# Low parts of the inner S sums taken out of the high-and-low split and written later in four pairs of a mixed FFT and gated MLP kernel

## The chip, the core and the metric

The kernel runs on one core of a Trainium2 chip. The metric is the time of one execution on the device in microseconds (us). The kernel before took 1030.15 us, the median of three runs (1030.04 to 1030.8).

## The reference

Two sublayers are computed from the same input `x` of 2048 rows by 640 columns, and mixed by a gate of one number a row. All arrays are float32.

```python
g = sigmoid((x * gate_w).sum(-1, keepdims=True))
a = dft_seq_re @ (x @ dft_hid_re.T) - dft_seq_im @ (x @ dft_hid_im.T)
b = (gelu(x @ w_gate) * (x @ w_up)) @ w_down
return g * a + (1 - g) * b
```

`w_gate` and `w_up` have 640 by 1728 numbers, `w_down` 1728 by 640, the sequence matrices 2048 by 2048.

## The kernel before

**Products in three passes.** The operands of TensorE (PE) have the type `float32r`. Each is kept as a high part, which ScalarE (ACT) makes by a copy to that type (`high`, L75), and a low part, which VectorE (DVE) makes as operand minus high part (`low`, L78). `mm3` (L86 to L88) issues high by high, high by low and low by high into one bank of 128 by 512 sums.

**Fewer products by sums.** Gate and up projections use a Strassen scheme of 2 by 2 blocks, so that seven block products do the work of eight. Its operands are sums of blocks: `S1` to `S4` of the weights, `T1` to `T4` of `x`. In the main part two hidden blocks are taken as one pair, and the same scheme is used once more on the sums of the outer scheme. `whole_pair` (L509) does that for the pairs p = 2, 3, 4 and 5, that is for the hidden blocks f = 5 to 12 (f = 2p + 1 and 2p + 2). Pair 1 and the blocks before it go through other functions, and so does everything behind the pairs: the down projection (`step_k`), the sequence transform and the last transform.

**What one pair does, in its program order.** `whole_pair` is a generator. It writes the products of one pair and yields a step number now and then, and its caller writes other work at these steps. The names that matter here:

- `va`, `xa` are two banks of running sums, `v00`, `v01`, `v10` and `X[..]` are banks that are copied from them by ACT (`seed`, L443), so that the sum can go on in two places. In the profile they read `pva`, `pxa`, `pv` and `px`.
- `s1[..]` (in the profile `s`) are copies of such banks in SBUF; DVE adds `v..` to them (`plus`, L530) and ACT applies the gelu (L533).
- `chain_parts` (L229) writes, at step 3, the sums of the raw weights of one block into `ws{f}r` (DVE, L241 to L245). It returns a function that writes the high part `ws{f}h` (ACT, 128 by 1024), the low part `ws{f}l` (DVE, 128 by 1024) and the same for a small sum `wd`. The caller calls it for the first block of the pair at step 7, and for the second at step 16.
- `fifth_parts` (L284) writes four small sums `fs` of the two blocks' `S1` (L290 to L293) at step 7, and its own returned function splits them into `fh` at step 10. `fh` is first used behind step 23.
- `load_cross(3, i)` (L326) loads 512 KB from memory into `xx`, at the steps 7, 10 and 16. SP issues it.
- At step 19 the caller issues loads for other stages (`extras`: sums of the down weights in `sum_wd`, with tiles `dr`, `da`, sums `d0s` to `d5s` and the store `wsd`; and rows of `x` for the gate, tiles `xz`). Their DVE work is written at the steps 29 and 38. The raw weights of the next pair are loaded at step 23 (`wa`, `wb`).

**Who sets the order.** Inside a pair only PE's order is fixed to that of the program (`in_order(PE)`). On ACT, DVE and SP a scheduler orders the instructions at build time by its own estimate of when each can run. In the trace each engine runs its list just as it stands, so that an instruction that waits holds up all behind it.

**Buffers.** Nearly all large tiles share one pool of 48 buffers of 4 KB a partition (tag `s4`): the sums and their high and low parts, the `xx` loads, the raw weights and the hidden activations `s5{f}`. A tile gets a buffer that the scheduler takes for free at that point of its plan, and its first write waits, by semaphores, until the last use of the buffer's former tile is over. For `s5{f}` the last use is a store to memory: `keep` (L332) has POOL store each finished 128 by 512 tile to `hA` or `hT`, 256 KB each. These stores come in a row at the end of every pair.

Of the kernel before, what the change touches and what calls it, by code (L numbers as in the profile page):

```python
# [30 lines left out]
def kernel(  # L31
# [33 lines left out]
    def slot(dt, shape, name):  # L65
        return pool.tile(shape, dt, tag="s4", name=name, bufs=48)

    def mtile(dt, name):
        return pool.tile([P, T], dt, tag="m", name=name, bufs=12)
# [4 lines left out]
    def high(hi, raw):  # L74
        nc.scalar.activation(hi, raw, AF.Copy)  # L75

    def low(hi, lo, raw):
        nc.vector.tensor_tensor(lo, raw, hi.bitcast(F32), op=ALU.subtract)  # L78

    def split(hi, lo, raw):  # L80
        high(hi, raw)
        low(hi, lo, raw)

    def mm3(ps, lhs, rhs, first, last):
        (lh, ll), (rh, rl) = lhs, rhs
        nc.tensor.matmul(ps, lh, rh, start=first, stop=False, skip_group_check=True)  # L86
        nc.tensor.matmul(ps, lh, rl, start=False, stop=False, skip_group_check=True)  # L87
        nc.tensor.matmul(ps, ll, rh, start=False, stop=last, skip_group_check=True)  # L88
# [39 lines left out]
    def at(hilo, i):  # L128
        h, l = hilo
        return h[:, i], l[:, i]  # L130

    def copy(src, name):
        m = mtile(F32, name)
        nc.scalar.activation(m, src, AF.Copy)
        return m
# [49 lines left out]
    def wchunk(name):  # L185
        return slot(F32, [P, 8, P], f"{name}r"), slot(F32R, [P, 8, P], f"{name}h"), slot(F32R, [P, 8, P], f"{name}l")

    def wsmall(dt, name):
        return pool.tile([P, 2, P], dt, tag="w", name=name, bufs=6)
# [40 lines left out]
    def load_raw(f):  # L230
        ra, rb = slot(F32, [P, 8, P], f"wa{f}"), wsmall(F32, f"wb{f}")
        nc.sync.dma_start(ra, wf[f - 1, :, :8])
        nc.sync.dma_start(rb, wf[f - 1, :, 8:])
        return ra, rb

    def chain_parts(f, raw, W):

        ra, rb = raw
        sm, *c = wchunk(f"ws{f}")
        g01, g23, u23 = ra[:, 0:2], ra[:, 2:4], ra[:, 5:7]  # L240
        tt(sm[:, 0:2], rb, u23, op=ALU.add)  # L241
        tt(sm[:, 4:6], g01, rb, op=ALU.subtract)
        tt(sm[:, 2:4], sm[:, 0:2], g01, op=ALU.subtract)
        tt(sm[:, 6:8], g23, sm[:, 2:4], op=ALU.subtract)
        tt(rb[:, 1], ra[:, 4], ra[:, 7], op=ALU.subtract)  # L245
        d = wsmall(F32R, f"wd{f}")
        W["raw"] = sm[:, 0:2]

        def parts():
            split(*c, sm)  # L250
            split(d[:, 0], d[:, 1], rb[:, 1])
            W["D"] = d[:, 0], d[:, 1]
            for i in range(2):
                for k in range(4):
                    W[f"S{k + 1}", i] = at(c, 2 * k + i)

        return parts

    def plain_parts(f, ra):
        a = slot(F32R, [P, 2, 4, P], f"wp{f}")  # L260
        split(a[:, 0], a[:, 1], ra[:, 4:8])
        W = {"g5": (a[:, 0, 0], a[:, 1, 0]), "u5": (a[:, 0, 3], a[:, 1, 3])}
        for i in range(2):
            W["A22", i] = a[:, 0, 1 + i], a[:, 1, 1 + i]
        return W
# [61 lines left out]
    def load_cross(J, i):  # L327
        tcross[J, i] = slot(F32R, [P, 2, T], f"xx{J}{i}")
        nc.sync.dma_start(tcross[J, i].bitcast(F32), xtd[J][:, {1: 0, 4: 1, 2: 2}[i]])
# [178 lines left out]
    def whole_pair(p, WP, Ws, raws):  # L508


        f = 2 * p + 1
        b = {J: {"b11": at(Bs[0][J, 1], 0), "b21": at(Bs[0][J, 1], 1), "b22": at(Bs[1][J, 1], 1), "t3": at(Bs[1][J, 1], 0)} for J in (1, 2)}
        b[3] = {"b11": at(Bs[0]["T1"], 0), "b21": at(Bs[0]["T1"], 1), "b22": at(Bs[1]["T1"], 1), "t3": at(Bs[1]["T1"], 0)}
        for J in (1, 2):
            for i in (1, 2, 4):
                c = tcross.pop((J, i))
# [5 lines left out]
        def prod(ps, i, a, b, tp):  # L522
            for d in range(2):
                mm3(ps, Ws[i][a, d], at(Bs[tp][b], d), False, True)

        def fifth(ps, i, w, t, tp):
            mm3(ps, Ws[i][w], at(Bs[tp][5], t), False, True)

        def plus(a, c):
            tt(a, a, c, op=ALU.add)  # L530
# [4 lines left out]
        def state(i, tp):  # L535
            s2[i, tp] = copy(X[i, tp], f"s2{f + i}_{tp}")
# [32 lines left out]
        plus(xa_, sx)  # L569
        X[1, 1] = xa_  # L570
        s1[1, 1] = copy(xa_, f"s111{p}")
        fifth(v01, 0, "g5", 0, 1)
        plus(s1[0, 1], v01)
        yield 13
# [7 lines left out]
        yield 16  # L582
        fifth(va, 1, "g5", 0, 1)
        plus(s1[1, 1], va)
        prod(X[0, 0], 0, "S2", "T2", 0)
        state(0, 0)
        plus(s1[1, 1], sv)
# [7 lines left out]
        for i in (1, 2, 4):  # L595
            c = tcross.pop((3, i))
# [399 lines left out]
    B, tiles, load, piece, tsum, his, lows = load_x(0)  # L996
# [27 lines left out]
    with in_order(ACT, DVE, PE, mybir.EngineType.SP):  # L1024
# [14 lines left out]
        B, tiles, load, piece, tsum, his, lows = load_x(1)  # L1039
# [50 lines left out]
    for f in (1, 2):  # L1090
        s5 = pair(F32, f"s5{f}")
        work = [gate_up(f, W, Bs[tp], tp, s5[:, tp]) for tp in range(2)]
        for step in range(7):
# [5 lines left out]
            if (f, step) == (2, 0):  # L1099
                raws = load_raw(3), load_raw(4)  # L1100
# [10 lines left out]
    Ws = [plain_parts(3 + i, raws[i][0]) for i in range(2)]  # L1111
    for i in (1, 2):
        for J in (2, 1):
            load_cross(J, i)
    chain_parts(3, raws[0], Ws[0])()
    p, f = 1, 3
    for J in (2, 1):
        load_cross(J, 4)
# [2 lines left out]
    for i in range(2):  # L1121
        s5 = pair(F32, f"s5{f + i}")
        work = [chain(f + i, Ws[i], Bs[tp], tp, s5[:, tp], X[i, tp], s1[i, tp]) for tp in range(2)]
        for step in range(4):
            for w in work:
                next(w)
            if (i, step) == (0, 0):
                chain_parts(f + 1, raws[1], Ws[1])()
            if (i, step) == (0, 1):
                xc[3] = cross_loads(3)  # L1130
            if (i, step) == (0, 3):
                t3[3] = cross_sums(3, xc[3])
            if (i, step) == (1, 1):
                split(Bs[1]["T1"][0][:, 0], Bs[1]["T1"][1][:, 0], t3[3])
            if (i, step) == (0, 1):
                for do in extras(1, 2):
                    do()
            if (i, step) == (0, 2):
                nraws = load_raw(f + 2), load_raw(f + 3)
            if (i, step) == (1, 0):  # L1140
                raws = nraws
                WP = pair_parts(2, raws[0][0], raws[1][0])
            if (i, step) == (1, 1):
                Ws = [plain_parts(f + 2 + i, raws[i][0]) for i in range(2)]
                for J in (2, 1):
                    load_cross(J, 1)
            if (i, step) == (1, 2):
                load_cross(2, 2)
            if (i, step) == (1, 3):
                load_cross(1, 2)  # L1150
    for p in range(2, NK):
        f = 2 * p + 1
        more = p < NK - 1
        for J in (2, 1):
            load_cross(J, 4)
        with in_order(PE):
            for u in whole_pair(p, WP, Ws, raws):
                if u == 3:
                    parts = [chain_parts(f + i, raws[i], Ws[i]) for i in range(2)]
                if u == 7:  # L1160
                    parts[0]()
                    parts.append(fifth_parts(p, *Ws))
                    load_cross(3, 1)
                if u == 10:
                    WP[3] = parts[2]()
                    load_cross(3, 2)
                if u == 16:
                    parts[1]()
                    load_cross(3, 4)
                if u == 19:  # L1170
                    todo = extras(1, 2)
                if u == 23 and more:
                    nraws = load_raw(f + 2), load_raw(f + 3)
                if u == 29:
                    for do in todo[:1]:
                        do()
                    todo = todo[1:] + extras(p > 2, 2)
                if u == 38:
                    for do in todo:
                        do()  # L1180
                if more:
                    if u == 47:
                        nWP = pair_parts(p + 1, nraws[0][0], nraws[1][0])
                    if u == 56:
                        nWs = [plain_parts(f + 2, nraws[0][0])]
                        for J in (2, 1):
                            load_cross(J, 1)
                    if u == 62:
# [88 lines left out]
    for i, (j, ri, b, sp) in enumerate(cseq):  # L1277
# [20 lines left out]
        if not b:  # L1298
# [17 lines left out]
            if lst:  # L1316
# [4 lines left out]
                for d in range(2):  # L1321
                    c = sv["c11", d]
# [76 lines left out]
    for i, (tp, b, p) in enumerate(useq[: 3 * ND]):  # L1399
# [95 lines left out]
    for t in range(2):  # L1495
        parts = 2 if t else 1
# [74 lines left out]
```

## Time and profile before

| | us |
|---|---|
| median of three runs | 1030.15 |
| the profiled execution, whole | 1027.66 |
| its span, first to last instruction | 1025.8 |
| PE busy | 1016.0 |
| DVE busy | 807.0 |
| ACT busy | 489.3 |
| POOL busy | 140.7 |

Times in views of the trace count from the start of the span. Pair 2 runs at about 145 to 190 us, pair 3 from 190 to 241, pair 4 from 241 to 291, pair 5 from there on. A row of a timeline is: start, duration, engine, line, operation, out<-in, shapes, and in brackets the idle time of the engine just before it and what ended it. Matmuls follow each other every 0.227 us at full clock and each is drawn 0.39 us long, so an unbroken row of them overlaps; PE busy time close to the span means that there are few gaps. Line numbers are those of the kernel before; in the changed kernel they are 4 to 12 higher.

### The profile page before, as it was taken

How to read it: one execution, taken by the hardware profiler on the slowest of the kernel's cores; microseconds unless marked ns; L12 is line 12 of the kernel's file. 1: busy time of each engine (PE TensorE's matmuls, PEld its weight loads, DVE VectorE, ACT ScalarE, POOL GpSimd, SP SyncE). 2: the span in 40 equal slices, each digit the busy share in tenths (PEclk: the TensorE clock that was granted, in tenths of full speed). 3: DMA queues.
4: the chain of work that ended last, by engine and by line, in shares of the span. 5: the costliest groups of instructions: out<-in, count | busy, mean ns of one | idle time of the engine just before them, and what ended most of it. 6: DMA issues, size and time to landing. Idle time of an engine off the chain costs nothing.

```text
span 1025.8 us, 13092 instructions
## 1 busy us (share of the span) xinstructions
PE 1016.0 (99%) x4488; PEld 838.5 (82%) x4488; DVE 807.0 (79%) x1134; ACT 489.3 (48%) x654; POOL 140.7 (14%) x251
## 2 busy tenths in 40 slices
PE   9999999999999999999999999999999999999998
PEld 7888888787888888888888888888888888888887
DVE  6998797778785958976898976796598769697784
ACT  5445365454455547566355343443444345365430
POOL 0123131212121200100010011102100200021013
PEclk9999999999999999999999999999999999999999
DMA  8368697878698988867856679667966777897748
GB/s 300 120 211 290 248 326 269 298 258 308 235 336 310 301 285 278 282 257 254 322 190 237 212 244 331 228 216 259 324 231 215 269 270 286 292 323 217 276 92 134
DMA packets 87666, 265.00 MB, mean 258 GB/s; under 512 B 11088, under 2 KB 19312, under 8 KB 87600
## 3 DMA queue, kind: packets, MB, share of 16 engines
q1 hardware_dynamic: 65392, 194.47, 55.6%
q0 software_dynamic: 22064, 69.50, 19.8%
q8 instruction: 35, 0.57, 0.2%
q14 instruction: 31, 0.25, 0.1%
q10 hardware_dynamic: 144, 0.20, 0.1%
HBM read 194.38 MB, written 69.75 MB: 257 GB/s over the span
## 4 chain that ended last, share of the span: by engine, by line
PE 81%; issue 13%; POOL 4%; DMA 1%; DVE 1%; ACT 0%; POOLq 0%; DVEq 0%; ACTq 0%
PE pX L86 3%; PE pX L87 3%; PE pX L88 3%; PE pL L87 3%; PE pL L88 3%; PE pL L86 3%; PE pZ L88 2%; PE pZ L87 2%; PE pZ L86 2%; PE pV L87 2%; PE pV L88 2%; PE pV L86 2%; POOL hA L332 2%; POOL hT L332 1%; PE pR L87 1%
## 5 line engine op out<-in xcount | busy, mean ns | idle before, releaser
L75 ACT ACTIVATE ch<-csa 128x1024 fp32r<-128x1024 f32 x32 | 34.0, 1063 | 85.7 <-DVE csa L815 69.2
L75 ACT ACTIVATE ch<-cra 128x1024 fp32r<-128x1024 f32 x32 | 33.9, 1058 | 47.7 <-DVE cl L78 22.4
L78 DVE TENSOR_TENSOR cl<-crb,ch 128x1024 fp32r<-128x1024 f32 x32 | 39.1, 1221 | 16.3 <-ACT ch L75 14.7
L78 DVE TENSOR_TENSOR cl<-cra,ch 128x1024 fp32r<-128x1024 f32 x32 | 39.1, 1223 | 15.5 <-ACT ch L75 10.2
L88 PE MATMUL pL<-ch,xal 128*128 128x512 f32 x128 | 49.8, 389 | 0.0
L87 PE MATMUL pL<-cl,xah 128*128 128x512 f32 x128 | 49.8, 389 | 0.0
L86 PE MATMUL pL<-ch,xah 128*128 128x512 f32 x128 | 49.3, 389 | 0.0
L75 ACT ACTIVATE ch<-crb 128x1024 fp32r<-128x1024 f32 x32 | 33.8, 1057 | 25.0 <-PE pL L87 8.6
L78 DVE TENSOR_TENSOR cl<-csb,ch 128x1024 fp32r<-128x1024 f32 x32 | 39.2, 1224 | 3.1 <-ACT ch L75 1.2
L332 POOL DMA_DIRECT2D hA<-s x48 | 26.1, 544 | 104.7 <-DVE s L685 71.8
L78 DVE TENSOR_TENSOR cl<-csa,ch 128x1024 fp32r<-128x1024 f32 x32 | 39.0, 1220 | 1.2 <-ACT ch L75 0.8
L75 ACT ACTIVATE ch<-csb 128x1024 fp32r<-128x1024 f32 x32 | 34.0, 1063 | 9.3 <-DVE csb L818 5.8
L78 DVE TENSOR_TENSOR kl<-kw,kh 128x1024 fp32r<-128x1024 f32 (+1 forms) x26 | 31.4, 1209 | 5.8 <-ACT kh L75 5.8
L684 ACT ACTIVATE s<-s 128x512 f32<-128x512 f32 x20 | 12.7, 633 | 48.5 <-DVE s L530 33.0
L75 ACT ACTIVATE kh<-kw 128x1024 fp32r<-128x1024 f32 (+1 forms) x26 | 27.1, 1042 | 11.1 <-DVE kw L873 7.1
L928 POOL DMA_DIRECT2D out<-ks x12 | 6.5, 540 | 166.7 <-DVE ks L927 166.1
L332 POOL DMA_DIRECT2D hT<-s x48 | 26.0, 541 | 20.1 <-DVE s L703 5.5
L814 DVE TENSOR_TENSOR csa<-cra 128x512 f32<-128x512 f32 x32 | 21.9, 685 | 8.2 <-DMA wsu<-u2s 4.7
L86 PEld LDWEIGHTS pL<-ch,xah 128*128 128x128 f32 x128 | 24.0, 188 | 5.0
L87 PEld LDWEIGHTS pL<-cl,xah 128*128 128x128 f32 x128 | 24.0, 188 | 5.0
L88 PEld LDWEIGHTS pL<-ch,xal 128*128 128x128 f32 x128 | 24.0, 188 | 5.0
L1273 POOL DMA_DIRECT2D uA<-c x8 | 4.3, 541 | 170.2 <-DVE c L1360 170.0
(3120 smaller groups left out, 3442.1 us busy)
## 6 DMA issues: line engine op xcount, KB each, us to landing
cra<-in_ct SPq DMA_DIRECT2D x64, 512.0 KB, 4.4
crb<-in_ct SPq DMA_DIRECT2D x64, 512.0 KB, 5.3
xx<-xtd SPq DMA_DIRECT2D x42, 512.0 KB, 5.2
hA<-s POOLq DMA_DIRECT2D x48, 256.0 KB, 4.8
hT<-s POOLq DMA_DIRECT2D x48, 256.0 KB, 5.8
kr<-hA SPq DMA_DIRECT2D x24, 512.0 KB, 7.4
kr<-hT SPq DMA_DIRECT2D x24, 512.0 KB, 6.2
ux<-uA SPq DMA_DIRECT2D x24, 512.0 KB, 5.0
```

What stands on the lines that cost most here:

```text
L75: nc.scalar.activation(hi, raw, AF.Copy)
L78: nc.vector.tensor_tensor(lo, raw, hi.bitcast(F32), op=ALU.subtract)
L86: nc.tensor.matmul(ps, lh, rh, start=first, stop=False, skip_group_check=True)
L87: nc.tensor.matmul(ps, lh, rl, start=False, stop=False, skip_group_check=True)
L88: nc.tensor.matmul(ps, ll, rh, start=False, stop=last, skip_group_check=True)
L332: nc.gpsimd.dma_start(to[:, i], src)
L684: nc.scalar.activation(s2, s2, AF.Gelu_apprx_tanh)
L814: tt(s1[:, 0], r1[:, 1], r1[:, 0], op=ALU.subtract)
L928: nc.gpsimd.dma_start(out[2 * tp + t, e], src)
L1273: nc.gpsimd.dma_start(to[:, i], src)
```

## The change

The function that `chain_parts` returned is cut in two, one for the high parts and one for the low parts. In the four calls of `whole_pair`:

- step 7: high parts of the first block, and `load_cross(3, 1)` as before;
- step 12, which is new and lies just ahead of the matmuls of `fifth(v01, ..)`: low parts of the first block, and `load_cross(3, 2)`, which stood at step 10;
- step 13: the four small sums of `fifth_parts`, which stood at step 7;
- step 16: high and low parts of the second block and `load_cross(3, 4)`, as before;
- step 17, which is new: the split of `fifth_parts`' sums, which stood at step 10.

Pair 1 calls both functions one behind the other, as before. No operation is added or taken away.

```diff
-        def parts():
-            split(*c, sm)
-            split(d[:, 0], d[:, 1], rb[:, 1])
+        def highs():
+            high(c[0], sm)
+            high(d[:, 0], rb[:, 1])
+
+        def lows():
+            low(*c, sm)
+            low(d[:, 0], d[:, 1], rb[:, 1])
             W["D"] = d[:, 0], d[:, 1]
...
-        return parts
+        return highs, lows
...
         s1[1, 1] = copy(xa_, f"s111{p}")
+        yield 12
         fifth(v01, 0, "g5", 0, 1)
         plus(s1[0, 1], v01)
         yield 13
...
         plus(s1[1, 1], va)
+        yield 17
         prod(X[0, 0], 0, "S2", "T2", 0)
...
                 if u == 7:
-                    parts[0]()
+                    parts[0][0]()
+                    load_cross(3, 1)
+                if u == 12:
+                    parts[0][1]()
+                    load_cross(3, 2)
+                if u == 13:
                     parts.append(fifth_parts(p, *Ws))
-                    load_cross(3, 1)
-                if u == 10:
+                if u == 16:
+                    for do in parts[1]:
+                        do()
+                    load_cross(3, 4)
+                if u == 17:
                     WP[3] = parts[2]()
-                    load_cross(3, 2)
-                if u == 16:
-                    parts[1]()
-                    load_cross(3, 4)
```

The order of PE's instructions is the same in both kernels. Those of ACT, DVE and SP move, and buffers are given out in another order. The rows below are the built program's. In brackets stand the semaphores that an instruction waits for: `DMASW` is the landing of a DMA that POOL issued (a store), `DMAHW` the landing of one that SP issued (a load), the others are engines; the number behind a tile's name is its number in the program.

ACT in pair 2, behind the copy `s1002` (that is `s1[0, 0]`), before:

```order
L75 ACTIVATE wd6_1413<-wb6_1155 128x128 [waits DMAHW0_49,DVE_49]
L443 ACTIVATE pv102_1457<-pva2_1376 128x512 [waits PE_49,Activation_49]
L533 ACTIVATE s1002_1434<-s1002_1434 128x512 [waits DVE_49]
L75 ACTIVATE fh2_1459<-fs2_1440 128x512 [waits DMAHW3_49,DVE_49]
L134 ACTIVATE s1012_1469<-px012_1428 128x512 [waits DMASW5_49,DMASW2_49,DVE_49]
L443 ACTIVATE px102_1474<-pxa2_1377 128x512 [waits PE_49,Activation_49]
L75 ACTIVATE ws6h_1406<-ws6r_1405 128x1024
```

The same place now:

```order
L75 ACTIVATE ws6h_1406<-ws6r_1405 128x1024 [waits DMASW5_49,DMASW0_49,DVE_49]
L447 ACTIVATE pv102_1450<-pva2_1376 128x512 [waits PE_49,Activation_49]
L537 ACTIVATE s1002_1434<-s1002_1434 128x512 [waits DVE_49]
L75 ACTIVATE wd6_1413<-wb6_1155 128x128 [waits DMAHW0_49]
L447 ACTIVATE px102_1462<-pxa2_1377 128x512 [waits PE_49,Activation_49]
L134 ACTIVATE s1012_1457<-px012_1428 128x512 [waits DMASW1_49,DVE_49]
```

The high part of the second block, `ws6h`, moved from behind the copies `pv102` and `px102` to ahead of both, and it now waits for stores: its buffer is the one that `s53` had. In the pairs 3, 4 and 5 `ws8h`, `ws10h` and `ws12h` moved to the same place, but wait for no store. `fh` moved behind the copies in all four pairs.

SP in pair 3, from the load behind `xx14` on, before:

```order
L329 DMA xx31_1865<-xtd3_128 128x1024 [waits DMAHW5_49,DMAHW1_49,PE_49]
L721 DMA da2_1937<-in_wd 128x256 [waits DMAHW2_49]
L233 DMA wb9_1960<-in_wf 128x256 [waits DMAHW3_49]
L233 DMA wb10_1964<-in_wf 128x256 [waits DMAHW4_49,DVE_49,Activation_49]
L329 DMA xx32_1882<-xtd3_128 128x1024
L721 DMA da3_2001<-in_wd 128x256 [waits DMAHW6_49,DVE_49]
L329 DMA xx34_1921<-xtd3_128 128x1024 [waits DMAHW7_49]
L720 DMA dr2_1936<-in_wd 128x1024 [waits DMAHW0_49,PE_49]
L765 DMA xz6_1940<-in_xz 128x640 [waits DMAHW1_49,PE_49]
```

The same place now:

```order
L333 DMA xx31_1858<-xtd3_128 128x1024 [waits DMASW4_49,DMAHW1_49,DMASW0_49,DVE_49]
L333 DMA xx32_1889<-xtd3_128 128x1024 [waits DMAHW2_49,PE_49,Activation_49]
L333 DMA xx34_1918<-xtd3_128 128x1024 [waits DMAHW3_49,DMASW7_49,DMASW5_49]
L727 DMA da2_1937<-in_wd 128x256 [waits DMAHW4_49]
L233 DMA wb9_1960<-in_wf 128x256 [waits DMAHW5_49]
L233 DMA wb10_1964<-in_wf 128x256 [waits DMAHW6_49,DVE_49,Activation_49]
L727 DMA da3_2001<-in_wd 128x256 [waits DMAHW7_49,DVE_49]
L726 DMA dr2_1936<-in_wd 128x1024 [waits DMAHW0_49,PE_49]
L771 DMA xz6_1940<-in_xz 128x640 [waits DMAHW1_49,PE_49]
```

`xx31` now has the buffer that `s55` had and `xx34` that of `s56`, so both wait for stores at the head of SP's list, and everything behind them waits with them. Before, `ws7l` (DVE) had the buffer of `s55`; it has another now and waits for no store. `xz6` waits for `DMAHW1`, which in both kernels is the landing of `xx31`. Pair 4 has the same shape with `xx31`, `xx34`, `s57`, `s58` and `xz10`.

DVE in pair 3, where the sums `d2s`, `d3s` of the down weights stand among the adds that PE needs, before and now:

```order
L714 TENSOR_TENSOR d2s_1994<-dr2_1936,d2s_1994 128x256 [waits DVE_49]
L530 TENSOR_TENSOR s57_1794<-s57_1794,px003_1808 128x512 [waits DMAHW5_49,Activation_49]
L711 TENSOR_TENSOR d3s_2049<-da3_2001,dr3_2000 128x256 [waits DMAHW6_49,DMAHW5_49,PE_49]
L712 TENSOR_TENSOR d3s_2049<-dr3_2000,da3_2001 128x256
L530 TENSOR_TENSOR pza3_1967<-pza3_1967,sz3_1977 128x512 [waits Activation_49]
```

```order
L720 TENSOR_TENSOR d2s_1994<-dr2_1936,d2s_1994 128x256 [waits DVE_49]
L534 TENSOR_TENSOR s57_1794<-s57_1794,px003_1808 128x512 [waits Activation_49]
L717 TENSOR_TENSOR d3s_2049<-da3_2001,dr3_2000 128x256 [waits DMAHW5_49,DMAHW7_49,DMASW0_49,DVE_49]
L718 TENSOR_TENSOR d3s_2049<-dr3_2000,da3_2001 128x256
L719 TENSOR_TENSOR d3s_2049<-d3s_2049,dr3_2000 128x256 [waits DVE_49]
L772 ISA xz8_2004,z_68<-xz8_2004,gwb_69 128x640 [waits DMAHW6_49]
```

`d3s` now has the buffer of `d2s`, which has that of `xz6`. So `d2s` cannot start before `xz6` was used, and `d3s` not before `d2s` is stored (`DMASW0`). The adds to `pza` and `pz01`, for which PE waits, stand behind `d3s`. In pair 4 `d5s`, `d4s` and `xz10` stand in the same way.

More of the change, by code (lines that the diff above doesn't have):

```diff
@@ L1114 @@
             load_cross(J, i)
-    chain_parts(3, raws[0], Ws[0])()
+    for do in chain_parts(3, raws[0], Ws[0]):
+        do()
     p, f = 1, 3
@@ L1127 @@
             if (i, step) == (0, 0):
-                chain_parts(f + 1, raws[1], Ws[1])()
+                for do in chain_parts(f + 1, raws[1], Ws[1]):
+                    do()
             if (i, step) == (0, 1):
@@ L1160 @@
                 if u == 7:
-                    parts[0]()
-                    parts.append(fifth_parts(p, *Ws))
-                    load_cross(3, 1)
-                if u == 10:
+                    parts[0][0]()
[4 more added lines that the diff above has]
+                if u == 13:
+                    parts.append(fifth_parts(p, *Ws))
+                if u == 16:
+                    for do in parts[1]:
+                        do()
+                    load_cross(3, 4)
+                if u == 17:
                     WP[3] = parts[2]()
-                    load_cross(3, 2)
-                if u == 16:
-                    parts[1]()
-                    load_cross(3, 4)
                 if u == 19:
```

## The prediction

> **What bounds the kernel now.** First the page's table of engines, then the list of waits for PE.
>
> ```profile
> PE 1016.0 (99%) x4488; PEld 838.5 (82%) x4488; DVE 807.0 (79%) x1134; ACT 489.3 (48%) x654; POOL 140.7 (14%) x251
> PE px L86 <- ACT px L443: 4.6, 2, 2.3
> ```
>
> PE is busy for 1016.0 of 1025.8 us. As the change gives PE the same instructions in the same order, it can move the time only through gaps of PE and through its clock. The list of waits shows one group worth having: PE waited twice for a bank copied by ACT, 4.6 us together. The timelines of PE, DVE and ACT show where.
>
> ```profile
> 203.46 0.50 PE L86 MATMUL px<-xx,vq 128*128 128x512 f32 x1 [2.27 <-ACT px L443]
> 253.24 0.50 PE L86 MATMUL px<-xx,vq 128*128 128x512 f32 x1 [2.29 <-ACT px L443]
> 198.42 1.23 DVE L78 TENSOR_TENSOR ws7l<-ws7r,ws7h 128x1024 fp32r<-128x1024 f32 x1 [2.85 <-DMA hT<-s]
> 201.37 0.69 DVE L530 TENSOR_TENSOR px<-px,sx 128x512 f32<-128x512 f32 x1
> 202.34 0.58 ACT L134 ACTIVATE s<-px 128x512 f32<-128x512 f32 x1
> 202.82 0.59 ACT L443 ACTIVATE px<-pxa 128x512 f32<-128x512 f32 x1
> 248.19 1.23 DVE L78 TENSOR_TENSOR ws9l<-ws9r,ws9h 128x1024 fp32r<-128x1024 f32 x1 [2.81 <-DMA hT<-s]
> ```
>
> One gap lies in pair 3 and one in pair 4, at the same instruction. Read backwards: PE's matmul into `px10` starts when ACT has copied that bank (202.82 + 0.59); the copy stood behind `s<-px`, which needed DVE's add of 201.37; and DVE was late because `ws7l` waited 2.85 us for a store to `hT`, since its buffer had belonged to `s55`. The gap is a wait for a buffer whose old content is still being stored.
>
> The windows show what the second gap cost besides (the last row is the core's span and mean clock):
>
> ```profile
> 254.00:256.00 2.00, 2.00 (x6) 1.51 (x5) 2.00 (x4) 1.66 (x4) 0.00 (x0) 0.54 1.01 375
> 256.00:258.00 2.00, 2.00 (x7) 1.59 (x6) 1.64 (x3) 0.76 (x2) 0.00 (x0) 0.60 1.00 395
> core 0: 1025.8 us, clock 0.998
> ```
>
> The granted clock (third number from the end) fell to 0.54 and 0.60 in two windows of 2 us, that is 0.92 + 0.80 = 1.7 us lost. The first gap, as long, had no such stretch: the mean clock of the span is 0.998, and 1.7 of 1025.8 us is all of that.
>
> **What the change removes.** In the new order `px10` is copied ahead of `s1[0, 1]`, and `ws7l` and `ws9l` have buffers that wait for no store. So both gaps go, and the slow stretch with them: 2.27 + 2.29 + 1.7 = 6.3 us. Were that all, the kernel would be faster. But the stores are as late as before; the tiles that now get their buffers are others, and I follow what these hold up.
>
> **What it adds in pair 2.** Now `ws6h` waits for the last store of `s53`, and it stands on ACT ahead of the copy `pv10`.
>
> ```profile
> 152.44 0.39 PE L86 MATMUL pv<-xx,vq 128*128 128x512 f32 x1
> 148.02 1.04 ACT L75 ACTIVATE ws5h<-ws5r 128x1024 fp32r<-128x1024 f32 x1
> 150.65 0.58 ACT L443 ACTIVATE pv<-pva 128x512 f32<-128x512 f32 x1 [0.39 <-PE pva L88]
> L332 POOL DMA_DIRECT2D hT<-s x1: 540/540/540, 148.0 to 148.0; - x1
> DMA to landing us min/median/max: 7.3/7.3/7.3
> 156.50 1.23 DVE L78 TENSOR_TENSOR ws6l<-ws6r,ws6h 128x1024 fp32r<-128x1024 f32 x1 [1.06 <-ACT s L533]
> ```
>
> That store was issued at 148.03 and landed 7.3 us later, at 155.3. With an allowance of 0.1 for the wake-up ACT begins `ws6h` at 155.4; 1.0 for it (as `ws5h`) and 0.58 for `pv10` give 157.0. PE wanted `pv10` at 152.44 and had it since 151.2. So PE stands still for about **4.6 us**. Queued behind `ws6h` on ACT are also the gelu, `px10` and three copies; on DVE `ws6l` (1.23 us) runs once `ws6h` is there, ahead of the add to `px01`, four small sums and four adds. PE wants bank `px00` again for S3 after 24 matmuls (24 x 0.227 = 5.4 us) from 157.0, at 162.4; the ACT chain of some eleven instructions, with two gelus that need those adds, reaches the copy that frees it at about 163.3. That is **0.8 us** more. Pair 2 costs 5.4 us; bounds are a store that lands 2 us earlier or 1 us later (xx32's 512 KB now move beside it): 3.4 to 6.4.
>
> **What it adds in pair 3.** SP's list begins with `xx31`, which waits for `s55`, and `xx34`, which waits for `s56`. The times below are those of before; pair 2's delay moves all of them alike.
>
> ```profile
> L332 POOL DMA_DIRECT2D hT<-s x1: 540/540/540, 193.6 to 193.6; - x1
> DMA to landing us min/median/max: 8.0/8.0/8.0
> L329 SPq DMA_DIRECT2D xx<-xtd x1: 319/319/319, 194.4 to 194.4; - x1
> DMA to landing us min/median/max: 7.0/7.0/7.0
> 202.86 0.88 SPq L765 DMA_DIRECT2D xz<-in_xz  x2
> 209.36 0.83 DVE L766 CUSTOM_DVE_ANT_0 xz<-xz,gwb 128x640 f32<-128x640 f32 x1 [1.47 <-DMA xz<-in_xz]
> 210.87 0.42 DVE L711 TENSOR_TENSOR d2s<-da,dr 128x256 f32<-128x256 f32 x1 [0.67 <-PE pze L88]
> 213.45 0.55 POOL L715 DMA_DIRECT2D wsd<-d2s  x1 [19.27 <-DVE d2s L714]
> ```
>
> `s55` landed at 198.4 (the row of `ws7l`), so `xx31` is issued there and not at 194.42; `s56` landed at 193.64 + 8.0 = 201.6, and only then come `xx34`, `da2`, `wb9`, `wb10`, `da3`, `dr2`. `xz6` cannot go before `xx31` has landed, 7.0 us behind its issue: 205.4 and not 202.86. With the same flight it lands 2.5 us later, so DVE handles it at 211.8. `d2s` and its store follow as before but without the 0.67 us for PE: 213.45 + 2.5 - 0.7 = 215.2 for the issue. DVE then stops at `d3s` until that store has landed, L us later.
>
> ```profile
> DMA to landing us min/median/max: 2.9/3.6/6.9
> 216.99 0.43 DVE L711 TENSOR_TENSOR d3s<-da,dr 128x256 f32<-128x256 f32 x1 [1.40 <-PE pza L88]
> 219.34 0.70 DVE L530 TENSOR_TENSOR pz<-pz,sz 128x512 f32<-128x512 f32 x1
> 220.07 0.60 ACT L625 ACTIVATE s<-pz 128x512 f32<-128x512 f32 x1 [0.82 <-DVE pz L530]
> 221.55 0.39 PE L86 MATMUL pz<-x122h,ws7h 128*128 128x512 f32 x1
> ```
>
> The first of these rows is for the six `wsd` stores (123 to 272 us). From the start of `d3s` to the end of ACT's copy of `pz01` it took 3.7 us; with one small sum more in between (0.34) and the wake-up, PE can go on 4.1 us behind the landing: 215.2 + L + 4.1. PE arrives there at 221.55 - 2.27 = 219.3, its old gap being gone. The new gap is therefore L itself: 2.9 to 6.9 us. I take the median, **3.6**. Should the queue, which stood still meanwhile, deliver `xz6` with a flight of 3.7 and not 6.5, it would be 0.8; that is the lower end.
>
> **Pair 4** goes the same way, one pair on:
>
> ```profile
> 252.63 0.85 SPq L765 DMA_DIRECT2D xz<-in_xz  x2
> 259.04 0.82 DVE L766 CUSTOM_DVE_ANT_0 xz<-xz,gwb 128x640 f32<-128x640 f32 x1 [1.36 <-DMA xz<-in_xz]
> 272.65 0.39 PE L86 MATMUL pz<-x122h,ws9h 128*128 128x512 f32 x1
> ```
>
> `xx31` goes at 248.1 (the store that `ws9l` waited for), `xz10` 7.0 later at 255.1 and not at 252.63; DVE handles it at 261.5, the store of `d4s` is issued 3.4 later as in pair 3, at 264.9, and PE needs the result at 272.65 - 2.29 - 1.7 = 268.7: 264.9 + L + 4.1 - 268.7 = L + 0.3. With the median this is **3.9 us**, bounds 1.1 to 7.2. In pair 5 `xx32` waits for a store of `s59`, but no down-weight sums stand behind it, and nothing of PE's does: nothing.
>
> **Clock.** Three new gaps of 4.6, 3.6 and 3.9 us stand where two of 2.3 us gave one slow stretch of 1.7. I count two such stretches, 3.4 us; bounds are none and three, 0 to 5.1. [...]
>
> **Sum.** 5.4 + 3.6 + 3.9 + 3.4 - 6.3 = +10.0 us. The profiled execution took 1027.66 us, 1.9 more than its span, and the median of the runs is 2.5 above that; the difference is added to the median: 1030.15 + 10.0 = 1040.1, forecast **1040 us**. Three conditions carry it: the buffers as the built program gives them, stores as slow as in the trace, and L near its median.
>
> **Rivals.**
> - *Only pair 2's wait is left*: SP's loads, held back while the stores land, then fly faster, and the `d3s` and `d5s` waits are over before PE comes. 5.4 + 1.7 - 6.3 = +0.8: 1031, from 1028 to 1033. For it: pair 3's lower end is 0.8. Against it: flights of 6 to 7 us in every such burst of the trace.
> - *The long end*: L is 6.9 us, as it was for the very store of `d2s`. 5.4 + 6.9 + 7.2 + 5.1 - 6.3 = +18.3: 1048.
> - *Faster*: in pair 2 the last store of `s53` lands before PE comes for `pv10`. It would have to land by 150.8, 4.5 us earlier than in the trace, as ACT needs 1.6 us behind it; then the two old gaps are gained and, with pairs 3 and 4 hidden, 1030.15 - 6.3 + 0.8 = 1024.5. Against it: the stores before and behind this one took as long (the median of the six `hT` stores around it is 7.9 us).
>
> ```profile
> hT<-s POOLq DMA_DIRECT2D x6, 256.0 KB, 7.9
> ```
>
> - *The change doesn't reach the old wait*: DVE still holds `ws7l` first in its list and stalls there. Against it: its buffer now comes from `xx22`, which PE had finished. It would give 1030 to 1035.
>
> **How the numbers follow.** Forecast 0.56 (own range 1034 to 1046), only pair 2 0.20, the long end 0.16, faster 0.06, the old wait 0.02. 0.2% is 2.1 us, about what a measurement of this kernel can tell from no change. Faster than 1028.1: the fourth case and a little of the second, 0.08. Between: most of the second and the last, 0.13. Slower: 0.79. The range for 8 times in 10 takes in the forecast, most of the second case and the lower half of the third: 1029.5 to 1047.
>
> **What would show it.** In the changed kernel's list of waits PE should no longer wait for ACT's `px` at `L86` in pairs 3 and 4. It should wait once for `pv` at about 152 us, with ACT's `ws6h` idle before it by a store to `hT`; and twice for ACT's `s` ahead of `pz<-x122h`, with DVE's `d3s` and `d5s` idle by the store `wsd`. The forecast is wrong if `ws6h` starts before 151, if `xz6` lands early enough that `d2s` is stored by the time PE reaches S4, or if stores land 2 us sooner throughout.

## The result, and the profile after

The changed kernel took 1040.53 us, the median of four runs (1036.54 to 1041.49); the kernel before, in the runs beside it, 1030.47 us (1030.04 to 1030.96). The ratio is 1.009, with a 95% interval from 1.0063 to 1.0117. The change made the kernel about 1% slower. The profiled execution of the changed kernel was the shortest of its four, 1036.54 us with a span of 1034.7.

The page's table of engines (busy us, share of the span, instructions):

```profile
PE 1019.0 (98%) x4488; PEld 840.7 (81%) x4488; DVE 807.6 (78%) x1134; ACT 489.1 (47%) x654; POOL 140.7 (14%) x251
```

The list of waits of PE (us in total, times, the longest):

```profile
PE pz L86 <- ACT s L631: 5.7, 2, 3.2
PE pv L86 <- ACT pv L447: 4.6, 1, 4.6
```

The old group, PE waiting for ACT's copy of `px`, is gone. Two new groups stand in its place, with three waits. PE's timeline shows where they lie:

```profile
157.45 0.80 PE L86 MATMUL pv<-xx,vq 128*128 128x512 f32 x1 [4.65 <-ACT pv L447]
228.48 0.50 PE L86 MATMUL pz<-x122h,ws7h 128*128 128x512 f32 x1 [3.18 <-ACT s L631]
279.81 0.50 PE L86 MATMUL pz<-x122h,ws9h 128*128 128x512 f32 x1 [2.48 <-ACT s L631]
```

One gap in each of the pairs 2, 3 and 4, 10.3 us together; pair 5 has none. The first is explained by two rows of ACT:

```profile
155.86 1.06 ACT L75 ACTIVATE ws6h<-ws6r 128x1024 fp32r<-128x1024 f32 x1 [5.58 <-DMA hT<-s]
156.82 0.58 ACT L447 ACTIVATE pv<-pva 128x512 f32<-128x512 f32 x1
```

ACT stood still for 5.58 us ahead of `ws6h`, until a store to `hT` had landed. The copy `pv10` was next in its list, and PE started when that was done. For the second gap the rows of DVE, POOL and ACT belong together (pair 3, in order of time):

```profile
216.08 0.82 DVE L772 CUSTOM_DVE_ANT_0 xz<-xz,gwb 128x640 f32<-128x640 f32 x1 [4.63 <-DMA xz<-in_xz]
219.53 0.55 POOL L721 DMA_DIRECT2D wsd<-d2s  x1 [19.67 <-DVE d2s L720]
224.42 0.42 DVE L717 TENSOR_TENSOR d3s<-da,dr 128x256 f32<-128x256 f32 x1 [4.69 <-DMA wsd<-d2s]
227.83 0.60 ACT L631 ACTIVATE s<-pz 128x512 f32<-128x512 f32 x1 [4.99 <-DVE pz L534]
```

DVE handles `xz6` at 216.08, POOL stores `d2s` at 219.53, and DVE does nothing for 4.69 us until that store has landed and `d3s` may overwrite the buffer. The adds to `pza` and `pz01` are queued behind it, ACT waits for them, and PE for ACT. Pair 4 repeats it with `d4s` and `d5s`:

```profile
267.01 0.82 DVE L772 CUSTOM_DVE_ANT_0 xz<-xz,gwb 128x640 f32<-128x640 f32 x1 [3.52 <-DMA xz<-in_xz]
270.45 0.54 POOL L721 DMA_DIRECT2D wsd<-d4s  x1 [17.55 <-DVE d4s L720]
275.75 0.43 DVE L717 TENSOR_TENSOR d5s<-da,dr 128x256 f32<-128x256 f32 x1 [4.54 <-DMA wsd<-d4s]
```

The windows of the trace, cut where the granted clock changes, show what each gap cost besides (the granted clock is the third number from the end):

```profile
157.44:160.85 3.41, 3.40 (x8) 2.75 (x9) 3.41 (x9) 2.38 (x5) 0.00 (x0) 0.50 0.70 226
229.12:232.53 3.41, 3.41 (x10) 2.64 (x9) 3.21 (x9) 1.70 (x3) 0.10 (x1) 0.50 0.55 160
280.32:283.73 3.41, 3.41 (x9) 2.65 (x9) 3.12 (x9) 1.57 (x2) 0.00 (x0) 0.50 0.53 149
```

Each gap is followed by 3.41 us at half clock, in which PE does the work of 1.7. So the list of waits and the clock nearly make up the difference: 4.65 + 3.18 + 2.48 + 3 x 1.7 = 15.4 us of new loss, less the 6.3 that went, is +9.1, and the spans differ by 1034.7 - 1025.8 = 8.9. (Both sums leave something out; see **What went** below.)

### The profile page after: what moved, and what is told of

It reads as the page before. It is cut to its first block, busy times and chain, and to the rows that moved or that the text cites. A ratio compares the mean times of both kernels' runs of the same rounds, so it can differ in the third digit from the quotient of the medians.

```text
span 1034.7 us, 13095 instructions
## 1 busy us (share of the span) xinstructions
PE 1019.0 (98%) x4488; PEld 840.7 (81%) x4488; DVE 807.6 (78%) x1134; ACT 489.1 (47%) x654; POOL 140.7 (14%) x251
## 4 chain that ended last, share of the span: by engine, by line
PE 79%; issue 15%; POOL 4%; DVE 1%; DMA 1%; ACT 0%; POOLq 0%; DVEq 0%
PE pX L86 3%; PE pX L87 3%; PE pX L88 3%; PE pL L86 3%; PE pL L87 3%; PE pL L88 3%; POOL hT L336 2%; PE pZ L86 2%; PE pZ L87 2%; PE pZ L88 2%; POOL hA L336 2%; PE pV L86 2%; PE pV L87 2%; PE pV L88 2%; PE pY L86 1%
## 5 line engine op out<-in xcount | busy, mean ns | idle before, releaser
L75 ACT ACTIVATE kh<-kw 128x1024 fp32r<-128x1024 f32 (+1 forms) x26 | 27.0, 1040 | 10.6 <-DVE kw L879 6.7
```

## The experiments

The diffs are against the changed kernel. In them, `behind(a, b)` tells the scheduler to keep the instruction `a` behind `b` on their engine; it adds no wait of its own. `last()` is the instruction written last. As the scheduler plans anew, buffers may be given out anew too, so each expectation names those that matter. The ratios are to 13 runs of the kernel before on the same chip for each half of the table; the median of these is 1029.56 us for `a_ws6h`, `d_lows34`, `d_lows_h` and `c_lows_only`, and 1029.47 for the other four.

| run | median us | ratio to before, 95% interval | PE's gaps over 1 us in the pairs 2 to 5 (profiled execution) |
|---|---|---|---|
| a_ws6h | 1036.27 | 1.0062, 1.0045 to 1.0079 | 1.83, 3.39, 4.32 |
| d_lows34 | 1028.72 | 0.9992, 0.9983 to 1.0001 | 4.85 |
| d_lows_h | 1023.86 | 0.9943, 0.9929 to 0.9958 | 1.90 |
| c_lows_only | 1038.60 | 1.0085, 1.0070 to 1.0100 | 1.57, 4.09, 3.44, 1.52 |
| c_fifth_only | 1042.92 | 1.0138, 1.0109 to 1.0166 | 4.91, 1.16, 1.17, 5.36, 1.15, 1.61 |
| after_again | 1040.41 | 1.0111, 1.0080 to 1.0141 | 5.83, 4.27, 2.94 |
| a_h | 1024.32 | 0.9953, 0.9938 to 0.9968 | 1.42 |
| e_late6 | 1020.67 | 0.9921, 0.9897 to 0.9945 | none |

### Pair 2: the wait of ws6h moved behind the copies (a_ws6h)

```diff
         def highs():
             high(c[0], sm)
+            if (f - 1) // 2 in (2,) and f % 2 == 0:
+                behind(last(), marks["px10"])
...
         X[1, 0] = seed(xa_, f"px10{p}")
+        marks["px10"] = last()
```

> The changed kernel, with one instruction moved on ACT in pair 2 alone: ws6h, the high part of the second block, is held behind the copy px10 (and so behind pv10, too). It keeps the buffer of s53; in the pairs 3 and 4 buffers and order stay those of the changed kernel. Theory (three gaps with three causes of their own; in pair 2 it is the copy pv10 queued behind ws6h's wait for the store): the 4.65 us gap at pv<-xx,vq and the 1.7 us lost at half clock behind it go, the gaps at pz<-x122h,ws7h and pz<-x122h,ws9h stay at 2 to 5 us each: 1040.5 - 6.3 = 1034, from 1033 to 1036. Rival (the wait only moves: gelu, px00's copy and the adds behind ws6h are then late in its place): PE waits 4 us or more a little later in pair 2, at S3, and the time stays at 1039 to 1041.

Measured: 1036.27 us, 4.3 less than the changed kernel. ACT's row of `ws6h` in the timeline:

```profile
157.75 1.06 ACT L75 ACTIVATE ws6h<-ws6r 128x1024 fp32r<-128x1024 f32 x1 [3.16 <-DMA hT<-s]
```

PE's list of waits:

```profile
PE pz L86 <- ACT s L643: 7.7, 2, 4.3
PE px L86 <- ACT s L143: 1.8, 1, 1.8
```

`ws6h` still waits for the store, and starts no sooner. But `pv10` now stands ahead of it, and the gap of 4.65 us at `pv<-xx,vq` is gone. What the wait holds up now are the copies of `s`, and PE meets it at S3, for 1.8 us. Both expectations saw a part of it: the theory is right on the gap, the rival on the direction, though not on the size. The time is 0.3 above the theory's range, as it had no term for this.

### Pairs 3 and 4: is it d3s, or SP's held loads? (d_lows34)

```diff
         def lows():
             low(*c, sm)
+            if (f - 1) // 2 in (3, 4):
+                behind(last(), marks["px01"])
...
         plus(X[0, 1], sx)
+        marks["px01"] = last()
```

> The changed kernel, with one instruction moved on DVE in each of the pairs 3 and 4: the low part of the first block's sums (ws7l, ws9l) is held behind the add to px01. The buffers that follow from it: xx31 and xx34 still get those of s55 and s56 (s57 and s58 in pair 4), so that SP's list is held as in the changed kernel; but d2s gets xx31's and d3s fh3's, so that neither waits for xz6 nor for the store wsd (d4s and d5s alike). Pair 2 stays as it is. Theory (the gaps of the pairs 3 and 4 are d3s and d5s waiting for their neighbours' stores; SP's hold alone costs nothing): both gaps and the half clock behind them go, 3.2 + 2.5 + 2 x 1.7 = 9.1: 1040.5 - 9.1 = 1031.4, from 1030 to 1034, with the 4.65 us gap of pair 2 left. Rival (it is SP's held loads, with xz6 and the down weights landing late): the gaps at pz<-x122h stay at 2 us or more in both pairs, and the time at 1037 to 1041.

Measured: 1028.72 us, 11.8 less than the changed kernel and below the theory's range. The 9.1 us came from the shortest execution; the second profile of the changed kernel (below) has 4.27 + 2.94 us of gaps in these pairs and 1.5 + 3.1 us lost to half clock behind them, 11.8. The whole list of PE's waits in the pairs is now one line:

```profile
PE pv L86 <- ACT pv L458: 4.8, 1, 4.8
```

The timelines of pair 3 have SP's `xx31`, DVE's `xz6`, POOL's store of `d2s`, and DVE's `d3s`:

```profile
205.56 0.32 SPq L344 DMA_DIRECT2D xx<-xtd  x1
217.68 0.83 DVE L784 CUSTOM_DVE_ANT_0 xz<-xz,gwb 128x640 f32<-128x640 f32 x1 [3.27 <-DMA xz<-in_xz]
221.01 0.55 POOL L733 DMA_DIRECT2D wsd<-d2s  x1 [18.86 <-DVE d2s L732]
223.83 0.42 DVE L729 TENSOR_TENSOR d3s<-da,dr 128x256 f32<-128x256 f32 x1
```

SP's queue is held as long as in the changed kernel (there `xx31` was issued at 204.63), `xz6` comes no sooner (there 216.08), and DVE still waits 3.27 us for it. Yet PE has no gap. What is different is `d3s`: it starts 2.8 us behind the issue of the store of `d2s`, and waits for nothing. (In this kernel the add to `pza` also stands ahead of `d3s`; the run with only the high parts moved, below, has it behind `d3s` as in the changed kernel, and no gap either.) So the rival falls: the held loads cost nothing by themselves. The gaps of the pairs 3 and 4 are `d3s` and `d5s` waiting for a store of their neighbour.

### Both moves, in all pairs (d_lows_h)

The two diffs above with `(2, 3, 4, 5)` in both conditions.

> Both of these moves together and in all four pairs: the low part of the first block behind the add to px01, the high part of the second block behind the copy px10. Theory (with no copy and no down-weight sum queued behind a wait for a store, neither the old gaps nor the new ones are left): 1030.5 - 6.3 = 1024, with 1 to 3 us for new small waits 1024 to 1027, faster than both kernels. Rival (writing the low parts and the small sums later costs by itself, since they crowd DVE and ACT ahead of S2 and S3): new gaps of 2 us or more in every pair, 1029 or over.

Measured: 1023.86 us, 0.57% faster than before. One gap is left in the pairs, by PE's list of waits:

```profile
PE px L86 <- ACT s L143: 1.9, 1, 1.9
```

The later places of the low parts and of the small sums, which this run has in common with the changed kernel, make no gaps. The rival falls.

### One part of the change at a time (c_lows_only, c_fifth_only)

First the low parts of the first block alone, then the small sums of `fifth_parts` alone:

```diff
                 if u == 7:
                     parts[0][0]()
+                    parts.append(fifth_parts(p, *Ws))
                     load_cross(3, 1)
+                if u == 10:
+                    WP[3] = parts[2]()
+                    load_cross(3, 2)
                 if u == 12:
                     parts[0][1]()
-                    load_cross(3, 2)
-                if u == 13:
-                    parts.append(fifth_parts(p, *Ws))
...
-                if u == 17:
-                    WP[3] = parts[2]()
```

> One part of the change alone: the low parts of the first block at step 12, while the four small sums and their split stand at the steps 7 and 10 and the S1 loads at 7, 10 and 16, as before. The buffers that follow: ws5l gets that of s53, xx31 those of s55 and s57, xx34 none of a store's, d3s that of d2s and d5s that of d4s. Theory (gaps follow who gets a buffer that is still being stored): ws6h does not wait, so the 4.65 us gap is gone (1 to 2 us may come at S3, as DVE waits in ws5l); d3s and d5s wait for their neighbours' stores as in the changed kernel, 2 to 5 us each and 1.7 behind each: 1024 + 1.5 + 2 x (3 to 5) + 2 x 1.7 = 1035 to 1039. Rival (it is the later place of the small sums, absent here, that brings the cost): no gap at pz<-x122h, 1024 to 1030.

```diff
                 if u == 7:
-                    parts[0][0]()
+                    for do in parts[0]:
+                        do()
                     load_cross(3, 1)
-                if u == 12:
-                    parts[0][1]()
+                if u == 10:
                     load_cross(3, 2)
```

> The other part of the change alone: the four small sums of S1 at step 13, their split at 17 and the S1 loads at 7, 12 and 16, while the low parts of the first block stay at step 7. The buffers that follow: ws6h again gets that of s53 and stands ahead of pv10; xx31 none of a store's; ws7l those of s55 and ws9l of s57; d2s gets xx31's (no wait for xz6), but d3s that of d2s; the pair 4 alike. px10's copy no longer stands behind that of px01, so the two gaps of before at px<-xx,vq should go here, too. Theory: pair 2 as in the changed kernel, 4.65 + 1.7 to 2.4; d3s and d5s wait for wsd, but one or two us sooner, as d2s doesn't wait for xz6: 1 to 4 us each; 1 us or so at S3, since DVE waits in ws7l. From 1024: 6.5 + 2 x (1 to 4) + 2 + 2 = 1036 to 1042. Rival (only both parts together bring d3s's wait, through xz6): no gap at pz<-x122h, 1030 to 1033.

In the second kernel the middle load stands at step 10, as the diff has it, not at 12 as the expectation says. Measured: 1038.60 and 1042.92 us, the second 0.9 above its range. The low parts alone cost 9.0 us over the kernel before, the small sums alone 13.5, both together 10.9 (in the next run): the costs do not add up. In the kernel with the low parts alone DVE waits in `ws5l`, ahead of PE's matmul that needs it:

```profile
156.98 1.23 DVE L78 TENSOR_TENSOR ws5l<-ws5r,ws5h 128x1024 fp32r<-128x1024 f32 x1 [4.09 <-DMA hT<-s]
```

PE's list of waits has that, for 1.6 us, and two waits at `pz<-x122h`:

```profile
PE pz L86 <- ACT s L631: 7.5, 2, 4.1
PE px L88 <- DVE ws5l L78: 1.6, 1, 1.6
```

With the small sums alone, `ws7l` waits for `s55` again, as before, and `d3s` for the store of `d2s`, issued here at 223.66:

```profile
206.58 1.23 DVE L78 TENSOR_TENSOR ws7l<-ws7r,ws7h 128x1024 fp32r<-128x1024 f32 x1 [3.53 <-DMA hT<-s]
230.56 0.42 DVE L717 TENSOR_TENSOR d3s<-da,dr 128x256 f32<-128x256 f32 x1 [6.71 <-DMA wsd<-d2s]
```

PE's list of waits again has the two at `pz<-x122h`, the longer one in pair 3:

```profile
PE pz L86 <- ACT s L631: 7.0, 2, 5.4
```

Both rivals fall, and the long gaps stand where the buffers said. Not all of the two expectations held, though. With the small sums alone the two gaps of before at `px<-xx,vq` were to go, and they stayed, with 1.16 and 0.82 us: the copy of `px10` no longer stands behind `s<-px`, but behind a gelu, which in pair 3 waits 2.71 us for DVE because of `ws7l`. With the low parts alone there is a gap of 1.52 us in pair 5, where DVE waits 2.71 us for a load of `xz`; no expectation had it. And the size of one gap was missed: I expected 1 to 4 us in pair 3 of the second kernel, because `d2s` no longer has the buffer of `xz6` and would be sooner, and the gap is 5.36. But `d2s` still stands behind `xz6` in DVE's list and was no sooner, and the flight of its store was 6.9 us (223.66 to 230.56).

### The changed kernel once more (after_again)

No edit.

> The changed kernel as it is, for a second profile: the first one's execution, 1036.5 us, was the shortest of four (the others 1040.5 to 1041.5). Theory (the gaps are the flights of stores, which vary): the same three places; in an execution of about 1040 us the gaps at pz<-x122h in the pairs 3 and 4 are longer than 3.2 and 2.5 us, together by 2 to 4, and half clock follows each gap for 3.4 us or twice that. Rival (something else than the gaps varies): the same gaps within 0.5 us each, and the rest elsewhere, as a new place of waiting.

Measured: 1040.41 us, the profiled execution 1040.43. PE's and DVE's timelines:

```profile
158.81 0.80 PE L86 MATMUL pv<-xx,vq 128*128 128x512 f32 x1 [5.83 <-ACT pv L447]
226.91 0.42 DVE L717 TENSOR_TENSOR d3s<-da,dr 128x256 f32<-128x256 f32 x1 [6.12 <-DMA wsd<-d2s]
230.98 0.79 PE L86 MATMUL pz<-x122h,ws7h 128*128 128x512 f32 x1 [4.27 <-ACT s L631]
282.52 0.79 PE L86 MATMUL pz<-x122h,ws9h 128*128 128x512 f32 x1 [2.94 <-ACT s L631]
```

The core's span and mean granted clock:

```profile
core 0: 1038.7 us, clock 0.992
```

The same three places, with 13.0 us of idle time in place of 10.3, and half clock for 6.83, 3.41 and 6.83 us. Some of that fell while PE was idle; what fell behind the gaps cost 1.77 + 1.52 + 3.07 = 6.36 us, in place of 5.12. 2.73 + 1.24 = 3.97 us, and the span is 3.93 longer: two thirds of the difference are in the gaps, one third in the clock. The gaps of the pairs 3 and 4 grew by 1.55 together, a little less than the 2 to 4 expected, and that of pair 2 by 1.18, which I had not named. The rival falls: no new place of waiting is there.

### Only the high parts moved, in all pairs (a_h)

The diff of the first experiment with `(2, 3, 4, 5)`.

> The changed kernel, with the high part of the second block held behind the copy px10 in all four pairs, and the low parts left to the scheduler. The buffers that follow: d2s gets xx31's and d3s fh3's (pair 4 alike), as in the run with both moves; xx31 and xx34 those of s55 and s56. Theory (gaps follow the buffers and what is queued behind their waits): no wait for wsd; pair 2 as in that run, about 1.9 at S3: 1024 to 1026. Rival (it was the place of the low parts that made the pairs 3 and 4 fast): gaps of 2 us or more at pz<-x122h, 1029 or over.

Measured: 1024.32 us; 0.46 us lie between this and the run with both moves, and their intervals overlap. The rival falls: the low parts need not be held. Pair 3 has, on POOL and DVE:

```profile
214.95 0.55 POOL L733 DMA_DIRECT2D wsd<-d2s  x1 [17.80 <-DVE d2s L732]
217.52 0.42 DVE L729 TENSOR_TENSOR d3s<-da,dr 128x256 f32<-128x256 f32 x1
217.86 0.69 DVE L545 TENSOR_TENSOR pza<-pza,sz 128x512 f32<-128x512 f32 x1
```

The store of `d2s` took 5.9 us and landed at 220.9; `d3s` ran 3.3 us ahead of that, with the adds to `pza` and `pz01` behind it as in the changed kernel. It is enough that the new plan gives `d3s` another buffer, which here came with the move of `ws8h` and was no aim of it.

### The second block's parts later in pair 2 (e_late6)

On top of the run with both moves:

```diff
-                behind(last(), marks["px10"])
+                behind(last(), marks["s200" if f == 6 else "px10"])
...
         state(0, 0)
+        marks["s200"] = last()
...
-                if u == 16:
+                if u == (19 if p == 2 else 16):
                     for do in parts[1]:
                         do()
+                if u == 16:
                     load_cross(3, 4)
```

> The run with both moves in all pairs (1023.9 us), with one further step in pair 2: the high and low parts of the second block are written at step 19 and held behind the copy that frees px00 for S3. Its buffer is then that of s54, and xx34 gets that of s53. Theory: the last gap of the main part, 1.9 us at px<-xT03h,ws5h, goes with the half clock behind it (1.4 to 1.7): 1023.9 - 3.5 = 1020.5, from 1020 to 1022.5. Rival (the wait comes back at the next use, as ws6h or its low part is late for PE, 8 us on): 1024 or over, with a gap at px<-xT02h,ws6h.

Measured: 1020.67 us, 0.8% faster than the kernel before (interval 0.5% to 1.0%) and 1.9% faster than the changed one. The page's table of engines:

```profile
PE 1013.3 (99%) x4488; PEld 837.7 (82%) x4488; DVE 806.2 (79%) x1134; ACT 490.5 (48%) x654; POOL 140.6 (14%) x251
```

ACT's timeline at `ws6h`:

```profile
157.23 1.05 ACT L75 ACTIVATE ws6h<-ws6r 128x1024 fp32r<-128x1024 f32 x1
```

The core's span and mean granted clock:

```profile
core 0: 1018.5 us, clock 1.000
```

`ws6h` has no idle time before it, because the stores have landed when its turn comes (the last of that row, to `hT`, at 156.2). PE's first matmul with it starts at 164.02, 5.7 us behind its end. No gap is left in the pairs, and the rival falls.

## Why the prediction was right

The forecast was 1040 us and the measured median is 1040.53; the forecast of +10.0 us stands against a difference of medians of 10.06. All three gaps were named with their place and their cause, and the experiments bear the causes out: the first move of `ws6h` for pair 2, the two runs in which `d3s` has another buffer for the pairs 3 and 4.

The agreement to a tenth of a us is luck. The two profiles of the changed kernel are 8.9 and 12.9 us longer than the one profile of before, and the medians are 10.06 apart because the median of before lies 2.8 us above its own profiled execution; no trace of a longer execution of before was kept. The single terms were off, too, and their errors cancelled in part: for the gaps 5.4 + 3.6 + 3.9 = 12.9 us were forecast and 10.3 and 13.0 measured, for the clock 3.4 against 5.1 and 6.4.

**What went.** Both old gaps and their stretch at half clock went, as predicted. 6.3 us was a little too small: matmul by matmul, the profile of before falls 7.3 us behind that of the last experiment within the pairs 2 to 4. Each gap cost 0.27 us more than its bracket says: 0.16 because the matmul ahead of it is drawn 0.39 us long where the next would start after 0.227, and 0.11 because the first matmul behind it takes 0.33. Some 0.4 more lie at four matmuls of the pairs 2 and 3 that the list of waits does not name. By the same measure the new losses of the first profile are 16.0 us and not 15.4, and 0.2 came ahead of the pairs: 16.0 - 7.3 + 0.2 = 8.9.

**Pair 2.** Predicted 4.6, measured 4.65 (5.83 in the second profile). The 0.8 us at S3 was not seen. The half clock behind the gap slowed PE by 1.7 us on its way to S3, more than the 0.8 by which ACT was to be late; I take that to have covered it, though no run tried it apart.

**Pair 3.** Predicted 3.6, measured 3.18 (4.27 in the second profile), by errors of opposite sign. The delay of pair 2 was 4.65 + 1.7 = 6.35 us, so the prediction's times shift by that. The store of `d2s` was forecast for 215.2 + 6.35 = 221.55 and issued at 219.53, 2.0 us sooner; its flight, L, was 4.9 (219.53 to 224.42) and not 3.6. The 3.6 was the wrong figure to take: it is the median of six stores in the profile of before, of which `d0s`, `d3s` and `d5s` took 2.9 us each, while the two that count here, `d2s` and `d4s`, took 6.9 and 4.7. SP's rows show where the 2.0 come from:

```profile
204.63 0.32 SPq L333 DMA_DIRECT2D xx<-xtd  x1
...
209.85 1.40 SPq L771 DMA_DIRECT2D xz<-in_xz  x2
```

`xx31` was issued at 204.63, against 198.4 + 6.35 = 204.75 forecast. But `xx31` flew 3.9 us, not 7.0, and `xz6` went 5.2 us behind its issue. (The flight of `xz6` itself was 6.2, about as long as before.) So the idea in the first rival, that loads held back fly faster, was right for `xx31`: alone it would have brought the gap down to 1.6 (3.6 - 2.0). The longer L gave 1.3 of it back, and PE came 0.35 sooner. From the landing on, the steps held: PE went on 4.06 us behind the start of `d3s`, forecast 4.1.

**Pair 4.** Predicted 3.9, measured 2.48 (2.94 in the second profile). The times shift by 6.35 + 3.18 + 1.7 - 2.27 = 9.0. The store of `d4s` was forecast for 273.9 and issued at 270.45, 3.4 sooner, as `xz10` again came sooner: `xx31` was issued 1.2 us ahead of its forecast, at 255.87, and `xz10` went 5.1 us behind it, not 7.0. L was 5.3 and not 3.6, which gave back 1.7, and PE came 0.3 sooner.

**Clock.** Predicted two stretches, 3.4 us; measured three, 5.1. This is the term with the wrong working: I counted by the two gaps of before, of which one (2.29 us) had such a stretch and the other (2.27 us) had none. All three new gaps had one, also the shortest, of 2.48 us. The last section shows how the idle time of these gaps lay in the traces.

**Rivals.** That only pair 2's wait is left: it fell, as both other gaps came. Half of its idea was right, but the sooner loads alone would not have closed the gaps: with L at 3.6 some 1.9 us (3.18 - 1.3) and 0.8 (2.48 - 1.7) would have been left. The long end: it fell for this profile, but in the second DVE waited 6.12 us for the store of `d2s`, and in the kernel with the small sums alone 6.71, so L does come near its 6.9. The faster case: the store of `s53` landed 5.58 us behind ACT's coming free, so nothing of it came true. That the change does not reach the old wait: it fell, both old gaps are gone.

## What to carry to other kernels

Where tiles share one pool, a move of a few instructions hands out all buffers anew, and its cost is found by asking of each tile that now waits for a store: what stands behind it on its engine, and when does PE need that. Here a long wait was free where only late work was queued behind it (SP's loads: in `d_lows34` `xx31` went at 205.56 and `xz6` held DVE up for 3.27 us, and pair 3 had no gap of PE), and cost most of its length where a short copy or add for PE was (in the first profile of the changed kernel ACT's 5.58 us ahead of `pv10` gave a gap of 4.65, DVE's 4.69 ahead of `pz01` one of 3.18). A writer whose buffer is still being stored belongs behind the short work, and in the order of the queue it can go as late as its own reader allows. That closed the gap of pair 2. In the pairs 3 and 4 it was another buffer for `d3s` and `d5s`, which came by chance with the same moves. Both together turned a loss of 1% into a gain of 0.8%.

## What the runs showed of the hardware

**Half clock came in stretches of 3.41 or 6.83 us.** In the first profile of the changed kernel they begin at 157.44, 229.12 and 280.32, which are 71.68 = 21 x 3.413 and 51.20 = 15 x 3.413 us apart; in the second, those at 230.62 and 281.82 are again 51.20 apart. Cutting a trace at these times into slices of 3.413 us, one can compare PE's idle time in a slice with the clock in the next. The kernel before, two slices and what follows each (PE's busy time is the second number, the granted clock the third from the end):

```profile
199.57:202.98 3.41, 1.62 (x8) 1.00 (x6) 3.11 (x11) 1.69 (x4) 0.00 (x0) 1.00 0.74 219
202.98:206.39 3.41, 2.93 (x13) 2.41 (x14) 3.41 (x5) 2.90 (x5) 0.00 (x0) 1.00 0.99 335
250.77:254.18 3.41, 1.12 (x5) 0.81 (x5) 3.11 (x8) 3.12 (x6) 0.00 (x0) 1.00 0.91 268
254.18:257.59 3.41, 3.41 (x10) 2.63 (x9) 3.38 (x5) 2.11 (x4) 0.00 (x0) 0.50 1.00 384
```

The gaps are as long as each other, 2.27 and 2.29 us. But the first lay across two slices, with 1.79 us idle in one and 0.48 in the next, and the clock stayed up; the second lay in one slice, and the clock fell. In the run with both moves the clock fell behind a little more than 1.79:

```profile
157.94:161.35 3.41, 1.51 (x8) 1.05 (x7) 2.82 (x4) 3.09 (x7) 0.00 (x0) 1.00 0.84 288
161.35:164.76 3.41, 3.41 (x10) 2.67 (x9) 1.42 (x3) 1.42 (x3) 0.00 (x0) 0.50 1.03 410
```

1.90 us idle, and the clock fell. In the first profile of the changed kernel the slices ahead of the three stretches have 3.41, 2.77 and 2.48 us of idle time; the two others that these gaps lie in have 1.22 and 0.41, and full clock behind them. In the second, 2.24 us (278.41 to 281.82) were followed by half clock; in the next slice, at half clock, 0.70 us were idle and half clock went on (this stretch lasts 6.83 us), while a slice at half clock with 0.36 us (230.62 to 234.03) was the last of its stretch. This is read from the traces, not tested with a kernel made for it, and a general border is not shown. For the three gaps that the prediction had, 4.6, 3.6 and 3.9, my estimate from these profiles would be three stretches, as the gaps of 4.65, 3.18 and 2.48 us had one each.

**A store of 512 KB took 2.9 us alone and up to 6.9 us among other transfers.** In the profile of before the stores of `d3s` and `d5s` landed in 2.9 us, and 178 to 181 GB/s moved meanwhile, which is those 512 KB and nothing else. Those of `d2s` and `d4s`, which had loads beside them (273 and 276 GB/s moved in the first 3 us of each), took 6.9 and 4.7 us there, and 4.9 and 5.3 in the first profile of the changed kernel; with the small sums alone that of `d2s` took 6.9, and DVE stood for 6.71 us. The changed kernel's executions differ by up to 5 us (1036.54 to 1041.49), those of the last experiment, with no wait for a store on PE's path, by 0.7 (1020.38 to 1021.03). That the stores make the difference is not shown: the four executions with the low parts alone, which wait for stores, differ by only 1.0 us.
